# Unit 0 in two halves of heads, an earlier weight piece, unit 5's attention moved with TensorE transposes, and the last tile in halves

## The chip, the core and the metric

The kernel runs on one core of a Trainium2 chip. The metric is the device time of one execution in microseconds; the kernel before took 304.26 us (median of 3 runs, 303.33 to 305.32) when the prediction was made. The "span" of a profile is the time from the first to the last instruction; the device time is about 2 us longer. A profile shows one execution only. In its lines PE is TensorE (PEld its weight loads), DVE VectorE, ACT ScalarE, POOL GpSimd and SP SyncE; L220 is line 220 of that run's kernel. A run is called slow here when it took over 1.5% more than the fastest run of the same kernel.

## The reference, cut to what matters

```python
# q, k, v: (8 batches, 8 heads, 576 positions, 64) fp32; chunks of 64 positions attend to themselves
scores = scale * q_c @ k_c.T                   # 64x64 per chunk and head
attn   = exp(scores - max) / sum
x      = (attn @ v_c) laid out as 4608 tokens x 512
h      = x @ w_in                              # 512 -> 2048
g      = h * sigmoid(beta * h)
out    = g @ w_out                             # 2048 -> 512
```

A *unit* is 256 tokens, a *block* is two units. The names below: `sc` the scores, `et` their exponential, `x` the attention product and its normalised copy, `xt` its transpose, `hps` the first product (16 *groups* m of 128 rows of w_in's output, 4 matmuls each), `gt` the gated result, `ops` the second product. *Scores 5* is the scores of unit 5, h6 the second half of columns of group 6, and a *PSUM tile* is one of the four buffers that groups, transposes and outputs share.

## The kernel before

Attention for the next units is laced between the matmuls of the current block by a list of positions. From block 1's second half on, x is transposed by DMA; the first four units are transposed by TensorE.

```python
    def emit_T(u, which=("kT", "qT")):      # VectorE transposes of k and q, 32x32 blocks
        ...
        loads_to(u + 4)                     # frees buffers: the loads of unit u+4 may go

    def emit_norm(u, s):                    # VectorE: reciprocal, then x * 1/sum -> x16
        ...
    def emit_xt_pe(u, s, on_act=True):      # 4 TensorE transposes, ScalarE copies them to xt
        ...
    def emit_xt_dma(u, s):                  # SyncE: DMA transpose x16 -> xt
        xf = x16_t.pop((u, s)).rearrange("p r h d -> p (r h d)")
        nc.sync.dma_start_transpose(out=xt_at(u, s), in_=xf)

    def emit_m(j, m, c0=0, n=None):         # one group: 4 matmuls, tanh on ScalarE, product on VectorE
        ...                                 # its PSUM tile comes from a pool of 4 (ps_p)

    with tc.manual_schedule():
        # unit 0: two loads by SyncE; the rest by GpSimd, in this order:
        # v of unit 0, q and k of unit 1, v of unit 1, 8 pieces of w_in, w_out, units 2, 3
        ...
        emit_idle(12, 512)                  # warm-up matmuls
        nc.scalar.copy(out=q_t[0], in_=raw0[0])
        nc.vector.tensor_copy(out=k_t[0], in_=raw0[1])
        emit_T(0, ("qT", "kT"))
        emit_sc(0, True)
        ...
        for j in range(1, NB):
            items = []
            if j == 1:
                items += [(0.03 * m, 0, ("h", m)) for m in range(9)]        # second half of columns
                items += [(0.30 + 0.10 * (m - 9), 0, ("m", m)) for m in range(9, KFF)]
                items += [(0.29, 3, ("T", 4))] + att_items(4, 0.45, 0.55)[:-1] + [(0.90, 3, ("T", 5))]
            else:
                m0 = 0.42 if j == 2 else 0.02
                ...
                if j == 2:
                    items += att_items(5, 0.01, 0.40)       # all of unit 5's attention
            ...                                             # emitted in order of position
        for t in range(4):
            emit_t(NB - 1, t)
```

The softmax here doesn't subtract the row's maximum and nothing guards it: scores larger than these inputs give would overflow.

Of the kernel before, what the change touches and what calls it, by code (L numbers as in the profile page):

```python
# [8 lines left out]
FP32 = mybir.dt.float32  # L9
FP16 = mybir.dt.float16  # L10
ACTF = mybir.ActivationFunctionType
ALU = mybir.AluOpType
# [3 lines left out]
def kernel(  # L16
# [14 lines left out]
    CH = 64  # L31
# [22 lines left out]

    ident = const.tile([128, 128], FP16)
    idle = const.tile([128, 512], FP16)
    raw0 = [const.tile([128, H, 2, D], FP32, name=f"raw{i}") for i in range(2)]
    braw = const.tile([128, 32], FP32)
    bt = const.tile([128, 32], FP32)
    beta2 = const.tile([128, KFF], FP32)  # L60
# [46 lines left out]
    def loads_to(u):  # L107
        while nxt[0] <= min(u, NU - 1):
            load_unit(nxt[0])
            nxt[0] += 1  # L110
# [31 lines left out]
    x_t = {}  # L142
    x16_t = {}
    xt_t = {}

    def emit_sc(u, split=False):
        qt, kt = qT.pop(u), kT.pop(u)
# [108 lines left out]
    def emit_idle(n, w):  # L256
        d = ps_p.tile([128, 512], FP32, tag="p", name="warm")
        for _ in range(n):
            nc.tensor.matmul(out=d[:, 0:w], lhsT=idle[:, 0:128], rhs=idle[:, 0:w])  # L259

    with tc.manual_schedule():
        nc.vector.memset(idle, 0.0)
        nc.vector.memset(braw, 0.0)  # L263
        nc.vector.memset(vbig[:, :, :, D:D + 1], 1.0)
        for i, src in enumerate((q, k)):
            nc.sync.dma_start(
                out=raw0[i],
                in_=src[0, :, 0:UNIT, :].rearrange("h (p r) d -> p h r d", r=2),
            )
        bv = moe_beta.rearrange("(m w f) -> w m f", w=4, f=32)  # L270
        for w in range(4):
            nc.sync.dma_start(out=braw[32 * w:32 * w + KFF, :], in_=bv[w])
        for dst, nm in ((q_t, "qu"), (k_t, "ku")):
            dst[0] = qk_p.tile([128, H, 2, D], FP16, tag=nm, name=nm)
        load_v(0)
        load_v(1)
        nxt[0] = 1
        loads_to(1)
        make_identity(nc, ident)
        for g in range(8):  # L280
            load_w_in(g)
        for g in range(3):
            load_w_out(g)
# [1 line left out]
        load_w_out(3)  # L285
        loads_to(3)

        emit_idle(12, 512)
        nc.scalar.copy(out=q_t[0], in_=raw0[0])
        nc.vector.tensor_copy(out=k_t[0], in_=raw0[1])  # L290
        emit_T(0, ("qT", "kT"))
        emit_sc(0, True)
        nc.vector.transpose(out=bt, in_=braw)
        nc.scalar.activation(out=beta2, in_=bt[:, 0:KFF], func=ACTF.Copy, scale=0.5)
        emit_idle(6, 128)
        emit_pv(0)
        emit_norm(0, 0)
        emit_norm(0, 1)
        emit_idle(8, 128)
        emit_xt_pe(0, 0)  # L300
        emit_xt_pe(0, 1)
        emit_T(1)
        emit_sc(1, True)
# [30 lines left out]
        emit_m(1, 0, 0, 256)  # L334
        emit_m(1, 1, 0, 256)
        emit_sc(3, True)
        for m in range(2, 6):
            emit_m(1, m, 0, 256)
        emit_pv(3)
        emit_norm(3, 0)  # L340
        emit_norm(3, 1)
        for m in range(6, 9):
            emit_m(1, m, 0, 256)
        emit_xt_pe(3, 0)
        emit_xt_pe(3, 1)

        def att_items(u, a0, w):
            return [(a0, 2, ("sc", u)), (a0 + 0.40 * w, 3, ("pv", u)),
                    (a0 + 0.41 * w, 3, ("norm", u, 0)), (a0 + 0.55 * w, 3, ("norm", u, 1)),
                    (a0 + 0.70 * w, 3, ("T", u + 1))]  # L350

        for j in range(1, NB):
            items = []
            if j == 1:
                items += [(0.03 * m, 0, ("h", m)) for m in range(9)]
                items += [(0.30 + 0.10 * (m - 9), 0, ("m", m)) for m in range(9, KFF)]
                items += [(0.29, 3, ("T", 4))] + att_items(4, 0.45, 0.55)[:-1] + [(0.90, 3, ("T", 5))]
            else:
                m0 = 0.42 if j == 2 else 0.02
                items += [(m0 + (1 - m0) * m / KFF, 0, ("m", m)) for m in range(KFF)]  # L360
                for t in range(4):
                    for hf in range(2):
                        items.append((0.98 * (t + 0.5 * hf) / 4, 1, ("t", t, hf)))
                if j == 2:
                    items += att_items(5, 0.01, 0.40)
                if j + 1 < NB:
                    if j == 2:
                        items += att_items(6, 0.40, 0.29) + att_items(7, 0.68, 0.26)
                    else:
                        for i in range(2):  # L370
                            items += att_items(2 * j + 2 + i, 0.03 + 0.43 * i, 0.43)
            items.sort(key=lambda it: it[:2])
            for _, _, it in items:
                if it[0] == "m":
                    emit_m(j, it[1])
                elif it[0] == "h":
                    emit_m(j, it[1], 256, 256)
                elif it[0] == "t":
                    emit_t(j - 1, it[1], 8 * it[2], 8 * it[2] + 8)
                elif it[0] == "sc":  # L380
                    emit_sc(it[1])
                elif it[0] == "pv":
                    emit_pv(it[1])
                elif it[0] == "norm":
                    emit_norm(it[1], it[2])
                    emit_xt_dma(it[1], it[2])
                elif it[1] < NU:
                    emit_T(it[1])
        for t in range(4):
            emit_t(NB - 1, t)  # L390


# [28 lines left out]
```

## Time and profile before

| what | value | from |
|---|---|---|
| span of the profiled execution | 303.2 us | head of the page |
| TensorE busy | 285.1 us, 94% | busy table |
| VectorE, ScalarE busy | 151.2, 147.3 us | busy table |
| mean granted clock of TensorE | 0.983 | result of that execution |
| chain that ended last: TensorE's share | 84% | chain of waits |

Two things are to be read from it. TensorE is the bound, and a bound engine can gain only where it stands still or runs slowly. A mean clock of 0.983 means that (1 - 0.983) x 303.2 / 0.5 = 10 us of this execution ran at half clock. Such stretches last 3.4 us or a multiple of it; 3.4 us is called a *window* below. The prediction below shows the lines of the slices, the stretches and the waits that say where.

### The profile page before, as it was taken

The numbers are of one execution on the slowest core, as the hardware profiler recorded it, in microseconds if no ns is written. First come the engines' busy times: TensorE is split into PE (matmuls) and PEld (weight loads), VectorE is DVE, ScalarE is ACT, GpSimd is POOL, SyncE is SP. The second block draws the span as 40 slices with busy tenths as digits, with TensorE's granted clock in tenths as the row PEclk, the third lists the DMA queues.
The fourth block names the chain that finished last, engine by engine and source line by source line (L and its number), as shares of the span: only waits on it lengthen the run. The fifth ranks groups of instructions, "written<-read, shape, count | busy, mean of one in ns | idle before, by whom it ended". The sixth has DMA issues, their size and how long they took to land.

```text
span 303.2 us, 7038 instructions
## 1 busy us (share of the span) xinstructions
PE 285.1 (94%) x2998; PEld 138.7 (46%) x2998; DVE 151.2 (50%) x272; ACT 147.3 (49%) x227; POOL 79.0 (26%) x104
## 2 busy tenths in 40 slices
PE   6789999798399999999999999999999999999995
PEld 2564446644134444444444444444444444444442
DVE  1577424776028755563647364736473635444300
ACT  3387228772227454545454545454545455544411
POOL 8843667644403340504060404000000000000000
PEclk9799999999869999999999999999999999999999
DMA  9999999999963992969196919411120212100011
GB/s 171 182 196 206 178 173 226 185 168 143 186 49 83 111 152 58 132 96 141 52 134 94 140 54 143 85 37 55 51 70 37 67 39 71 66 38 37 35 69 69
DMA packets 102046, 32.44 MB, mean 107 GB/s; under 512 B 89216, under 2 KB 97408, under 8 KB 102016
## 3 DMA queue, kind: packets, MB, share of 16 engines
q0 software_dynamic: 79392, 17.83, 64.2%
q1 hardware_dynamic: 22624, 14.17, 16.4%
q8 instruction: 23, 0.38, 0.5%
q14 instruction: 7, 0.06, 0.1%
HBM read 36.71 MB, written 9.44 MB: 152 GB/s over the span
## 4 chain that ended last, share of the span: by engine, by line
PE 84%; DVE 7%; DMA 4%; ACT 2%; issue 1%; SPq 0%; ACTq 0%; DVEq 0%
PE ops L242 40%; PE hps L220 38%; PE sc L153 4%; DVE gt L229 3%; DMA xt<-x 2%; DMA raw<-in_k_dram 2%; PE x L174 2%; DVE x L186 2%; DVE kT L132 1%; DVE qT L132 1%; ACT sg L228 1%; ACT xt L203 1%; PE xp L201 1%; DVE rd L184 0%; ACT osb L252 0%
## 5 line engine op out<-in xcount | busy, mean ns | idle before, releaser
L229 DVE SCALAR_TENSOR_TENSOR gt<-sg,hps 128x512 f16<-128x512 f32 (+1 forms) x159 | 100.2, 635 | 115.3 <-ACT sg L228 114.4
L220 PE MATMUL hps<-xt,win 128*128 128x512 f16 (+1 forms) x636 | 139.0, 363 | 5.9 <-DMA xt<-x 5.0
L228 ACT ACTIVATE sg<-hps,beta 128x512 f32<-128x512 f32 (+1 forms) x159 | 101.7, 647 | 84.0 <-PE hps L220 84.0
L242 PE MATMUL ops<-wout,gt 128*128 128x512 f16 x576 | 135.5, 382 | 0.0
L220 PEld LDWEIGHTS <-win 128*128 128x128 f16 x636 | 60.3, 98 | 65.3 <-issue 8.0
L242 PEld LDWEIGHTS <-gt 128*128 128x128 f16 x576 | 55.9, 98 | 67.4 <-issue 2.2
L252 ACT ACTIVATE osb<-ops 128x512 f32<-128x512 f32 x36 | 21.5, 597 | 44.8 <-PE ops L242 44.8
L87 POOL DMA_DIRECT2D qu<-in_q_dram x23 | 18.0, 787 | 89.3 <-DVE qT L132 85.4
L95 POOL DMA_DIRECT2D vbig<-in_v_dram x40 | 34.0, 866 | 10.5 <-DMA wout<-in_moe_w_out_dram 3.7
L162 ACT ACTIVATE et<-sc 128x1024 f16<-128x1024 f32 (+1 forms) x21 | 18.6, 901 | 17.6 <-PE sc L153 17.6
L186 DVE TENSOR_TENSOR x<-x,rd 128x512 f16<-128x512 f32 x36 | 24.9, 691 | 1.2
L87 POOL DMA_DIRECT2D ku<-in_k_dram x23 | 18.0, 789 | 2.1 <-DMA win<-in_moe_w_in_dram 1.5
L153 PE MATMUL sc<-qT,kT 32*64 32x64 f16 x1152 | 12.8, 193 | 4.7 <-DVE kT L132 2.7
L153 PEld LDWEIGHTS <-kT 32*64 32x64 f16 x1152 | 10.9, 107 | 12.3 <-DVE qT L132 4.8
L132 DVE STREAM_TRANSPOSE kT<-ku 128x512 f32<-128x512 f32 x18 | 12.7, 703 | 2.3 <-DMA ku<-in_k_dram 2.3
L184 DVE RECIPROCAL rd<-x 128x8 f32<-128x8 f32 x36 | 7.2, 200 | 10.3 <-PE x L174 10.3
L132 DVE STREAM_TRANSPOSE qT<-qu 128x512 f32<-128x512 f32 x18 | 12.1, 672 | 0.0
L174 PEld LDWEIGHTS <-et 64*64 64x64 f16 x576 | 6.5, 110 | 8.2 <-issue 3.7
L174 PE MATMUL x<-vbig,et 64*64 64x65 f16 x576 | 8.8, 198 | 0.8 <-issue 0.6
L259 PE MATMUL warm<-idle 128*128 128x128 f16 (+1 forms) x26 | 7.0, 455 | 1.2 <-DVE braw L263 1.2
L113 POOL DMA_DIRECT2D win<-in_moe_w_in_dram x8 | 6.1, 778 | 0.6 <-DMA ku<-in_k_dram 0.4
L203 ACT COPY xt<-xp 128x512 f16<-128x512 f16 x8 | 4.6, 584 | 2.6 <-PE xp L201 2.5
(18 smaller groups left out, 16.9 us busy)
## 6 DMA issues: line engine op xcount, KB each, us to landing
out_dram<-osb SPq DMA_DIRECT2D x36, 256.0 KB, 2.1
vbig<-in_v_dram POOLq DMA_DIRECT2D x32, 128.0 KB, 6.4
qu<-in_q_dram POOLq DMA_DIRECT2D x11, 256.0 KB, 5.2
ku<-in_k_dram POOLq DMA_DIRECT2D x11, 256.0 KB, 6.2
win<-in_moe_w_in_dram POOLq DMA_DIRECT2D x8, 256.0 KB, 10.1
wout<-in_moe_w_out_dram POOLq DMA_DIRECT2D x4, 512.0 KB, 12.6
qu<-in_q_dram POOLq DMA_DIRECT2D x4, 192.0 KB, 7.0
ku<-in_k_dram POOLq DMA_DIRECT2D x4, 192.0 KB, 7.4
```

The lines of the kernel that those rows point to most:

```text
L87: nc.gpsimd.dma_start(out=t[off // 2:(off + n) // 2], in_=src[b, :, s:s + n, :].rearrange("h (p r) d -> p h r d", r=2),)
L95: nc.gpsimd.dma_start(out=vbig[off:off + n, i, :, 0:D], in_=v[b, :, s:s + n, :].rearrange("h p d -> p h d"),)
L132: nc.vector.transpose(out=t.rearrange("p h s e -> p (h s e)").bitcast(FP32).rearrange("p (h i r) -> p h r i", h=H, r=2), in_=a.rearrange(" ...
L153: nc.tensor.matmul(out=sc[o0:o0 + 64, c // 2, h, :], lhsT=kt[p0:p0 + 32, h, :, e], rhs=qt[p0:p0 + 32, h, :, e], start=(e == 0), stop=(e == 1),
L162: nc.scalar.activation(out=et[:, s], in_=sc[:, s], func=ACTF.Exp, scale=scale)
L174: nc.tensor.matmul(out=x[64 * c:64 * c + 64, r, g, 0:D + 1], lhsT=et[64 * r:64 * r + 64, s, 4 * c + g, :], rhs=vbig[64 * r:64 * r + 64, i, ...
L186: nc.vector.tensor_tensor(out=x16, in0=x[:, :, :, 0:D], in1=rd.to_broadcast([128, 2, 4, D]), op=ALU.mult)
L220: nc.tensor.matmul(out=hps[:, 0:n], lhsT=w_in16[m // 2][:, kk, (m % 2) * 128:(m % 2) * 128 + 128], rhs=xr[:, c0 // CH:(c0 + n) // CH, 2 * ...
L228: nc.scalar.activation(out=sg[:, 0:n], in_=hps[:, 0:n], func=ACTF.Tanh, scale=beta2[:, m:m + 1])
L229: nc.vector.scalar_tensor_tensor(out=gt_t[j][:, m, c0:c0 + n], in0=sg[:, 0:n], scalar=1.0, in1=hps[:, 0:n], op0=ALU.add, op1=ALU.mult,)
L242: nc.tensor.matmul(out=ops, lhsT=gt_t[j][:, kk, t * 128:(t + 1) * 128], rhs=w_out16[kk // 4][:, kk % 4, :], start=(kk == 0), stop=(kk == K ...
L252: nc.scalar.activation(out=osb, in_=ops, func=ACTF.Copy, scale=0.5)
```

## The change

Its intent has four parts: start earlier by loading and transposing unit 0 in two halves of heads; bring the first weight piece ahead of unit 1's v; take unit 5 off the late DMA transpose by moving its attention (scores in block 1, the rest at the head of block 2, transposes on TensorE); end earlier by copying and storing the last tile in two halves.

```diff
+    def emit_T_half(a):       # casts and transposes of 4 heads
+    def emit_sc_half(a):      # scores and exponential of 4 heads
...
-        for i, src in enumerate((q, k)):
-            nc.sync.dma_start(out=raw0[i], in_=src[0, :, 0:UNIT, :]...)
+        for a in range(2):
+            for i, src in enumerate((q, k)):
+                nc.sync.dma_start(out=raw0[a][i], in_=src[0, HH * a:HH * a + HH, 0:UNIT, :]...)
...
-        nxt[0] = 1
-        loads_to(1)
+        load_qk(1)
+        load_w_in(0)
+        load_v(2)
+        load_v(3)
...
-        emit_idle(12, 512)
-        ...
-        emit_sc(0, True)
+        emit_idle(10, 512)
+        emit_T_half(0)
+        emit_sc_half(0)
+        emit_idle(8, 128)
+        emit_T_half(1)
+        emit_sc_half(1)
...
-        for m in range(2, 6):                # block 1, first half of columns: unit 3's product
+        for m in range(2, 5):                # one group earlier,
...
-        for m in range(6, 9):
+        for m in range(5, 10):               # two groups more before the second half
...
-                items += [(0.29, 3, ("T", 4))] + att_items(4, 0.45, 0.55)[:-1] + [(0.90, 3, ("T", 5))]
+                items += [(0.05, 3, ("T", 4)), (0.25, 2, ("sc", 4)), (0.42, 3, ("pv", 4)),
+                          (0.43, 3, ("norm", 4, 0)), (0.50, 3, ("norm", 4, 1)), (0.58, 3, ("T", 5)),
+                          (0.85, 3, ("sc", 5))]
...
-                    items += att_items(5, 0.01, 0.40)
+                    items += [(0.01, 3, ("pv", 5)), (0.02, 3, ("norm", 5, 0)), (0.06, 3, ("norm", 5, 1)),
+                              (0.13, 3, ("xp", 5, 0)), (0.19, 3, ("xp", 5, 1)), (0.20, 3, ("T", 6))]
...
-        for t in range(4):
+        for t in range(3):
             emit_t(NB - 1, t)
+        for hf in range(2):                  # last tile: 2 x 16 matmuls of 256 columns,
+            ...                              # copies on ScalarE and VectorE, stores by SyncE and ScalarE
```

More of the change, by code (lines that the diff above doesn't have):

```diff
@@ L56 @@
     idle = const.tile([128, 512], FP16)
-    raw0 = [const.tile([128, H, 2, D], FP32, name=f"raw{i}") for i in range(2)]
+    HH = H // 2
+    raw0 = [[const.tile([128, HH, 2, D], FP32, name=f"raw{i}{a}") for i in range(2)] for a in range(2)]
+    qk0 = [[const.tile([128, HH, 2, D], FP16, name=f"h0{i}{a}") for i in range(2)] for a in range(2)]
+    qkT0 = [[const.tile([128, HH, CH, 2], FP16, name=f"t0{i}{a}") for i in range(2)] for a in range(2)]
     braw = const.tile([128, 32], FP32)
@@ L144 @@
     xt_t = {}
+    def emit_T_half(a):
+        nc.scalar.copy(out=qk0[a][0], in_=raw0[a][0])
+        nc.vector.tensor_copy(out=qk0[a][1], in_=raw0[a][1])
+        for i in (0, 1):
+            nc.vector.transpose(
+                out=qkT0[a][i].rearrange("p h s e -> p (h s e)").bitcast(FP32).rearrange(
+                    "p (h i r) -> p h r i", h=HH, r=2),
+                in_=qk0[a][i].rearrange("p h r d -> p (h r d)").bitcast(FP32).rearrange(
+                    "p (h r i) -> p h r i", h=HH, r=2),
+            )
+    def emit_sc_half(a):
+        if a == 0:
+            et_t[0] = et_p.tile([128, 2, H, CH], FP16, tag="et", name="et")
+            x_t["s0"] = ps_s.tile([128, 2, H, CH], FP32, tag="s", name="sc")
+        sc = x_t["s0"]
+        qt, kt = qkT0[a]
+        for h in range(HH):
+            for e in range(2):
+                for c in range(4):
+                    p0, o0 = 32 * c, 64 * (c % 2)
+                    nc.tensor.matmul(
+                        out=sc[o0:o0 + 64, c // 2, HH * a + h, :],
+                        lhsT=kt[p0:p0 + 32, h, :, e],
+                        rhs=qt[p0:p0 + 32, h, :, e],
+                        start=(e == 0),
+                        stop=(e == 1),
+                    )
+        hs = slice(HH * a, HH * a + HH)
+        nc.scalar.activation(out=et_t[0][:, :, hs], in_=sc[:, :, hs], func=ACTF.Exp, scale=scale)
     def emit_sc(u, split=False):
@@ L264 @@
         nc.vector.memset(vbig[:, :, :, D:D + 1], 1.0)
-        for i, src in enumerate((q, k)):
-            nc.sync.dma_start(
-                out=raw0[i],
-                in_=src[0, :, 0:UNIT, :].rearrange("h (p r) d -> p h r d", r=2),
-            )
+        for a in range(2):
+            for i, src in enumerate((q, k)):
+                nc.sync.dma_start(
+                    out=raw0[a][i],
+                    in_=src[0, HH * a:HH * a + HH, 0:UNIT, :].rearrange("h (p r) d -> p h r d", r=2),
+                )
         bv = moe_beta.rearrange("(m w f) -> w m f", w=4, f=32)
@@ L272 @@
             nc.sync.dma_start(out=braw[32 * w:32 * w + KFF, :], in_=bv[w])
-        for dst, nm in ((q_t, "qu"), (k_t, "ku")):
-            dst[0] = qk_p.tile([128, H, 2, D], FP16, tag=nm, name=nm)
         load_v(0)
         load_v(1)
-        nxt[0] = 1
-        loads_to(1)
+        load_qk(1)
+        load_w_in(0)
+        load_v(2)
+        load_v(3)
+        nxt[0] = 2
         make_identity(nc, ident)
-        for g in range(8):
+        for g in range(1, 8):
             load_w_in(g)
@@ L286 @@
         loads_to(3)
-        emit_idle(12, 512)
-        nc.scalar.copy(out=q_t[0], in_=raw0[0])
-        nc.vector.tensor_copy(out=k_t[0], in_=raw0[1])
-        emit_T(0, ("qT", "kT"))
-        emit_sc(0, True)
+        emit_idle(10, 512)
[4 more added lines that the diff above has]
+        emit_sc_half(1)
         nc.vector.transpose(out=bt, in_=braw)
         nc.scalar.activation(out=beta2, in_=bt[:, 0:KFF], func=ACTF.Copy, scale=0.5)
-        emit_idle(6, 128)
+        loads_to(4)
+        emit_idle(8, 128)
         emit_pv(0)
@@ L298 @@
         emit_norm(0, 1)
-        emit_idle(8, 128)
+        emit_idle(12, 128)
         emit_xt_pe(0, 0)
+        emit_idle(4, 128)
         emit_xt_pe(0, 1)
@@ L341 @@
         emit_norm(3, 1)
-        for m in range(6, 9):
+        for m in range(5, 10):
             emit_m(1, m, 0, 256)
         emit_xt_pe(3, 0)
+        emit_m(1, 10, 0, 256)
         emit_xt_pe(3, 1)
@@ L354 @@
             if j == 1:
-                items += [(0.03 * m, 0, ("h", m)) for m in range(9)]
-                items += [(0.30 + 0.10 * (m - 9), 0, ("m", m)) for m in range(9, KFF)]
-                items += [(0.29, 3, ("T", 4))] + att_items(4, 0.45, 0.55)[:-1] + [(0.90, 3, ("T", 5))]
+                items += [(0.04 * m, 0, ("h", m)) for m in range(11)]
+                items += [(0.44 + 0.11 * (m - 11), 0, ("m", m)) for m in range(11, KFF)]
+                items += [(0.05, 3, ("T", 4)), (0.25, 2, ("sc", 4)), (0.42, 3, ("pv", 4)),
+                          (0.43, 3, ("norm", 4, 0)), (0.50, 3, ("norm", 4, 1)), (0.58, 3, ("T", 5)),
+                          (0.85, 3, ("sc", 5))]
             else:
-                m0 = 0.42 if j == 2 else 0.02
+                m0 = 0.27 if j == 2 else 0.02
                 items += [(m0 + (1 - m0) * m / KFF, 0, ("m", m)) for m in range(KFF)]
@@ L364 @@
                 if j == 2:
-                    items += att_items(5, 0.01, 0.40)
+                    items += [(0.01, 3, ("pv", 5)), (0.02, 3, ("norm", 5, 0)), (0.06, 3, ("norm", 5, 1)),
+                              (0.13, 3, ("xp", 5, 0)), (0.19, 3, ("xp", 5, 1)), (0.20, 3, ("T", 6))]
                 if j + 1 < NB:
                     if j == 2:
-                        items += att_items(6, 0.40, 0.29) + att_items(7, 0.68, 0.26)
+                        items += att_items(6, 0.32, 0.34) + att_items(7, 0.66, 0.30)
                     else:
@@ L385 @@
                     emit_norm(it[1], it[2])
-                    emit_xt_dma(it[1], it[2])
+                    if it[1] != 5:
+                        emit_xt_dma(it[1], it[2])
+                elif it[0] == "xp":
+                    emit_xt_pe(it[1], it[2])
                 elif it[1] < NU:
                     emit_T(it[1])
-        for t in range(4):
+        for t in range(3):
             emit_t(NB - 1, t)
+        for hf in range(2):
+            ops = ps_p.tile([128, DM], FP32, tag="p", name="ops")
+            for kk in range(KFF):
+                nc.tensor.matmul(
+                    out=ops[:, 0:256],
+                    lhsT=gt_t[NB - 1][:, kk, 384:512],
+                    rhs=w_out16[kk // 4][:, kk % 4, 256 * hf:256 * hf + 256],
+                    start=(kk == 0),
+                    stop=(kk == KFF - 1),
+                )
+            osb = osb_p.tile([128, DM], FP32, tag="osb", name="osb")
+            dst = out[NT - 128:NT, 256 * hf:256 * hf + 256]
+            if hf == 0:
+                nc.scalar.activation(out=osb[:, 0:256], in_=ops[:, 0:256], func=ACTF.Copy, scale=0.5)
+                nc.sync.dma_start(out=dst, in_=osb[:, 0:256])
+            else:
+                nc.vector.tensor_scalar(out=osb[:, 0:256], in0=ops[:, 0:256], scalar1=0.5, scalar2=None, op0=ALU.mult)
+                nc.scalar.dma_start(out=dst, in_=osb[:, 0:256])
 _INS = ['q', 'k', 'v', 'moe_w_in', 'moe_w_out', 'moe_beta']
```

## The prediction

> **What bounds the kernel now.** I read the busy table and the 40 slices first, then the waits, then the timeline around every place where TensorE isn't solid.
>
> ```profile
> PE   6789999798399999999999999999999999999995
> ...
> PEclk9799999999869999999999999999999999999999
> ```
>
> Each digit is a fortieth of 303.2 us, 7.58 us. From slice 13 (about 91 us) TensorE is full at full clock, so nothing can be won there except by removing work. The loss lies in the first slices and in the eleventh (75.8 to 83.4 us), where TensorE is busy 3 tenths; the granted clock is 8 and 6 tenths there and in the next slice. Busy time by stretch makes it exact (columns: length, busy time and count of PE, PEld, DVE, ACT, POOL, then clock, DMA share, GB/s):
>
> ```profile
> 60.00:77.00 17.00, 15.70 (x315) 7.70 (x312) 11.81 (x23) 8.01 (x12) 8.69 (x11) 1.00 1.71 162
> 77.00:82.10 5.10, 0.07 (x9) 0.03 (x1) 0.00 (x0) 1.09 (x2) 2.59 (x3) 0.91 1.79 165
> 82.10:88.50 6.40, 6.40 (x17) 2.25 (x18) 1.37 (x2) 1.37 (x2) 0.00 (x0) 0.54 1.13 102
> 88.50:96.00 7.50, 7.50 (x69) 3.31 (x71) 5.39 (x11) 4.03 (x6) 0.07 (x1) 1.00 0.18 45
> ```
>
> TensorE stands still for 5.0 us, then runs 17 matmuls of 512 columns in 6.40 us at about half clock. At the usual pitch (64 take 13.83 us in the chain: 0.216 us each) they'd take 3.67 us, so the hole costs 5.03 + 2.73 = **7.8 us**. The chain of waits names what ended it:
>
> ```profile
> 75.63 6.33 DMA xt<-x
> 81.97 0.14 issue
> 82.10 3.57 PE hps L220 x8
> ```
>
> That is unit 5's second transpose, by DMA. It needed 6.33 us to land where the median is 2.4 us (table of DMA issues), in a stretch whose DMA share is 1.79, with loads of unit 10 in flight. Block 2's first product needs it and nothing is left to run meanwhile. The waits between 45 and 90 us show the small ones:
>
> ```profile
> PE hps L220 <- DMA xt<-x: 5.0, 1, 5.0
> PE sc L153 <- DVE qT L132: 1.3, 2, 0.8
> PE xp L201 <- ACT xt L203: 0.7, 1, 0.7
> PE hps L220 <- ACT xt L203: 0.7, 1, 0.7
> ```
>
> At the start the chain is latency, not throughput:
>
> ```profile
> 1.26 5.70 DMA raw<-in_k_dram
> 6.98 0.78 DVE ku L290
> 7.76 0.62 DVE qT L132
> 8.38 0.60 DVE kT L132
> 9.03 0.77 PE sc L153 x64
> ```
>
> **What the Trainium skill says.** "TensorE: Matmul & The Clock Gate", Part 1: the clock falls to half after about one idle window of 3.4 us and comes back after a busy one; the windows run freely. The trace agrees: half clock from about 81.2 to 88.05 us, two windows. The same page, Architectural detail, says VectorE and ScalarE run their queues strictly in order, while TensorE only pulls weight loads ahead. The trace fits: the second transpose of unit 3 (54.45 us) started only after the product of group m = 6 (ended 54.42), which stood in VectorE's queue behind unit 3's normalisation. I use this below. "DMA: Bandwidth & Descriptors", Anatomy of one DMA, gives a fixed cost of about 2.0 us; this case's output stores take 2.1 us for 256 KB, so halving the last store saves only tenths.
>
> **The change part by part.**
>
> *First unit in halves.* In the trace q landed at 5.08 and k at 6.98 us. With half the heads each, q and k of the first half are as many bytes as q alone, so they should be there at about 5.1; the first half's scores fit under the second half's landing. After that landing remain half a cast (0.4), two half transposes (0.7), half the scores (0.4) and half an exponential (0.55) in place of 0.78 + 1.33 + 0.77 + 1.09: the attention product starts near 9.7 instead of 10.48 us. But 12 + 4 warm-up matmuls (about 0.1 us each) replace 8 ahead of the two transposes, so half of the 0.8 us goes back. More important, what follows waits for weights. The third group of the first block (m = 2) starts at 17.00, and GpSimd's wait for the second w_in piece ends at 16.98, the third at 18.04. Moving the first piece ahead of two v tiles brings that piece from about 14.5 to about 12 us, but the second piece has the same bytes ahead of it as before. Only the waits after 17.0 can go: 0.28 us before the second transpose of unit 1 and 0.24 us before the next groups, of which I count **0.2 us**.
>
> *End of block 1's first half.* Unit 3's normalisation comes after 5 products on VectorE (6 before), with 5 groups issued after the attention product (3 before). Four PSUM tiles serve groups and transposes, so the fifth group (m = 9) waits for the product of m = 5, which now stands behind both normalisations: 52.05 + 2 x 0.86 = 53.77, + 0.36 = 54.13, while TensorE is through at 52.9 to 53.0: 1.1 us. Then 0.9 us until unit 3's second copy ends and the second half of the columns starts, at about 56.73. Before, 1.65 us of waits and a start at 55.50 with two groups (0.86 us) fewer done: a loss of 1.23 - 0.86 = **0.4 us**.
>
> *Block 1's second half.* I count from H, its start, with the trace's pitches: TensorE 0.43 (256 columns) and 0.86 (512), ScalarE 0.44 and 0.69, exponential 1.02, VectorE 0.36 and 0.63 back to back, 1.33 for a pair of transposes, 0.86 for a normalisation. VectorE does h0 and h1 from H + 1.14 to 1.95, unit 4's transposes to 3.28, h2 at 3.63. Groups h2 to h5 fill the four tiles, so h6 starts at 3.65; scores 4 4.1 to 4.75, exponential to 5.87, then ScalarE's h7 to h10 to 7.6; VectorE follows: h10 8.03, normalisation 8.9, m11 9.5, normalisation 10.3, m12 10.9, unit 5's transposes 12.18. TensorE has done m14 at 10.4 and **waits 1.8 us** for scores 5. Then scores 12.87, m15 13.75, 8 output matmuls 15.48, attention product of unit 5 15.93, 8 more 17.66, eight TensorE transposes 18.45 (both normalisations end at 17.6), 8 output matmuls 20.2, by which time the copies (three ScalarE pieces of 0.6 from 17.75) have ended at 19.5. Block 2 starts at H + 20.2 = 76.93, or 76.73 with the 0.2 us of the start.
>
> *What that is worth.* At 88.47 us the old kernel has done 40 output matmuls of block 1, scores 6 and the first two groups of block 2. The new one at 76.73 lacks two groups (1.73), scores 6 (0.65) and 16 output matmuls (3.45): 82.56. Gain **5.9 us**, start included: the 7.8 us of the hole and the old small waits, less about 5 us of new waits and 0.8 us of transposes on TensorE. From there on the order is the same and TensorE is full in both.
>
> *Last tile in halves.* 32 matmuls of 256 columns: in the run of 64 that took 11.41 us, 40 of 512 leave 0.115 each, so 3.68 against 3.46 us: +0.2. The last copy is half as long (about 0.4 on VectorE against 0.60) and the last store carries 128 KB: -0.3. Net **-0.1 us**.
>
> Sum: 304.26 - 5.9 - 0.1 = **298.2 us**.
>
> **The rivals.**
>
> 1. *VectorE isn't late at scores 5.* Its work from H to the end of unit 5's transposes is 9.9 us without holes, TensorE's 9.3; my 12.2 contains the first latency (1.14) and a hole behind the exponential. If those overlap better than I walked them, the 1.8 us shrinks to about 0.5, and with the 1.1 us at m = 9 also smaller the time is 296. For it: the positions look tuned. Against: VectorE's strict order, as seen at unit 3.
> 2. *The clock drops in the new wait.* 1.8 us of idleness and 64 short matmuls fall near one window. At the start 2.66 us of idleness before such matmuls sufficed to halve the clock from about 9.6 to 12.9 us. If it happens, a window at half speed adds 1.7 us, two add 3.4: 300 to 301.5. The idle share is smaller than there, so I give it one chance in five.
> 3. *The hole moves to unit 4.* Its transposes remain DMAs, issued at about 65.7 and 67.2 us beside the loads of unit 8. At 6.3 us they'd land by 75, and block 2 wants them at 76.7. Slack of 2 us; a landing of 8 us or more would cost 1 or 2.
> 4. *The start gains its whole 0.8 us*, if the second weight piece lands earlier too: 297.6. I see no reason in the bytes.
>
> **The range and the chances.** The walk over some thirty steps may be off by 1 us either way, rival 1 pulls down by 2, rivals 2 and 3 up by 2 to 3. So 8 in 10 for 295.8 to 300.8. Faster by over 2% means below 298.2, which is my middle: 0.52 for faster, as rival 1 is a little likelier than 2 and 3 together, 0.47 within 2%, 0.01 slower.
>
> **What would show it.** The 5.0 us wait for the DMA should be gone and the clock at 1.00 from 60 to 100 us; scores 5 should wait 1 to 2 us for VectorE's transposes; group m = 9 of block 1 about 1 us; block 2 should start near 76.7 us and the solid stretch should end near 293.8 (299.5 - 5.9 + 0.2). Group m = 2 of block 0 should still start near 17 us, with the first scores near 6.5. I am wrong if the third group starts before 16.3, if the wait at scores 5 is under 0.5 us, if the clock falls after 60 us, or if unit 4's DMA appears in TensorE's waits.

## The result and the profile after

The changed kernel took **300.22 us** (median of 4 runs, 299.54 to 300.56), the kernel before 304.31 us (4 runs). A ratio is the mean time of one kernel's fast runs over that of the other's of the same rounds, so it is not quite the ratio of the medians: here 0.9863, 95% interval 0.9826 to 0.9899, within 2%. That lies in the predicted range of 295.8 to 300.8, 2.0 us above its middle.

The profiled execution took 299.54 us, span 297.7, mean clock 0.994. The slices of the page, busy tenths and granted clock:

```profile
PE   6689999787999999999999999999999999999995
...
PEclk9799999999999999999999999999999999999999
```

The slice with 3 tenths is gone, and so are the two with a clock of 8 and 6. What remains is 7, 8, 7 in slices 8 to 10 (52 to 74 us). The same stretches as in the prediction (length, busy time and count of PE, PEld, DVE, ACT, POOL, then clock, DMA share, GB/s), with the one before them:

```profile
60.00:70.00 10.00, 7.64 (x183) 4.63 (x185) 8.49 (x20) 6.47 (x12) 5.17 (x7) 1.00 2.01 167
...
77.00:82.10 5.10, 5.10 (x86) 2.50 (x85) 2.00 (x3) 2.98 (x4) 3.10 (x4) 1.00 1.35 154
82.10:88.50 6.40, 6.40 (x61) 2.95 (x60) 2.75 (x6) 3.02 (x5) 0.00 (x0) 1.00 0.75 98
```

Between 77 and 88.5 us TensorE now does nothing but work at full clock. In exchange it is idle 2.36 us between 60 and 70, where it was idle 1.30 us before (busy for 8.70 of these 10 us). Three of its waits up to 100 us (those of the first scores, 4.2 us in all, are part of the start below; the others are 1.2 us or less):

```profile
...
PE hps L254 <- DVE gt L263: 1.9, 2, 1.1
PE sc L187 <- DVE qT L135: 1.8, 2, 1.6
PE hps L254 <- ACT xt L237: 1.2, 2, 1.0
```

No DMA is in the list of TensorE's waits. VectorE is the new releaser, at m = 9, h6 and scores 5, three places that the prediction had walked. The timeline of TensorE there (start, length, line, operands, count, wait before it and its releaser; only the lines with a wait, and the first group of block 2):

```profile
54.95 0.60 PE L254 MATMUL hps<-xt,win 128*128 128x256 f16 x4 [1.12 <-DVE gt L263]
...
57.43 2.78 PE L254 MATMUL hps<-xt,win 128*128 128x256 f16 x24 [1.01 <-ACT xt L237]
...
61.01 0.60 PE L254 MATMUL hps<-xt,win 128*128 128x256 f16 x4 [0.79 <-DVE gt L263]
...
69.59 0.71 PE L187 MATMUL sc<-qT,kT 32*64 32x64 f16 x64 [1.56 <-DVE qT L135]
...
77.22 1.89 PE L254 MATMUL hps<-xt,win 128*128 128x512 f16 x8
```

From the start of block 1's second half (57.43) to block 2 (77.22) are 19.8 us; the prediction's walk had 20.2.

The start went the other way. The chain of waits of the changed kernel:

```profile
2.34 6.63 DMA raw<-in_k_dram
8.97 0.02 issue
8.99 0.43 DVE h L151
9.42 0.69 DVE t L153 x2
10.11 0.04 issue
10.16 0.45 PE sc L170 x32
```

The second half of k landed at 8.97 us; the whole k had landed at 6.96 before. The second half's scores began at 10.16 us, when all scores had already been begun at 9.03 before. Where block 0 takes up the second half of its columns, the loss can be read: first the kernel before, then the changed one (lines of the timeline up to 24 us).

```profile
20.14 4.08 PE L220 MATMUL hps<-xt,win 128*128 128x256 f16 x30 [0.24 <-ACT xt L203]
```

```profile
20.91 3.43 PE L254 MATMUL hps<-xt,win 128*128 128x256 f16 x27 [0.24 <-ACT xt L237]
```

The start is 0.77 us longer instead of 0.2 us shorter. In both executions the clock was at half for one window of the start (9.5 to 12.95 us before, 11.0 to 14.4 after), so this pair compares like with like.

### The profile page after: what moved, and what is told of

The parts are those of the page before. It is cut to its first block, busy times and chain, and to the rows that moved or that the text cites. A ratio compares the mean times of both kernels' runs of the same rounds, so it can differ in the third digit from the quotient of the medians.

```text
span 297.7 us, 7145 instructions
## 1 busy us (share of the span) xinstructions
PE 282.3 (95%) x3046; PEld 141.8 (48%) x3046; DVE 151.8 (51%) x278; ACT 148.6 (50%) x232; POOL 79.1 (27%) x104
## 4 chain that ended last, share of the span: by engine, by line
PE 88%; DVE 5%; DMA 2%; ACT 2%; issue 1%; SPq 0%; DVEq 0%; ACTq 0%
PE ops L276 41%; PE hps L254 39%; PE sc L187 4%; DMA raw<-in_k_dram 2%; PE x L208 2%; DVE gt L263 2%; DVE x L220 1%; PE ops L440 1%; ACT xt L237 1%; ACT sg L262 1%; DVE kT L135 1%; DVE qT L135 1%; PE xp L235 1%; SPq L301 0%; ACT et L196 0%
## 5 line engine op out<-in xcount | busy, mean ns | idle before, releaser
L276 PE MATMUL ops<-wout,gt 128*128 128x512 f16 x560 | 130.9, 379 | 0.0
L276 PEld LDWEIGHTS <-gt 128*128 128x128 f16 x560 | 54.0, 98 | 63.8
L286 ACT ACTIVATE osb<-ops 128x512 f32<-128x512 f32 x35 | 20.9, 597 | 42.1 <-PE ops L276 42.1
L196 ACT ACTIVATE et<-sc 128x1024 f16<-128x1024 f32 (+1 forms) x19 | 17.5, 933 | 11.9 <-PE sc L187 11.9
L187 PEld LDWEIGHTS <-kT 32*64 32x64 f16 x1088 | 10.2, 106 | 8.5 <-DVE qT L135 5.1
L187 PE MATMUL sc<-qT,kT 32*64 32x64 f16 x1088 | 12.1, 192 | 1.8 <-DVE qT L135 1.8
L135 DVE STREAM_TRANSPOSE kT<-ku 128x512 f32<-128x512 f32 x17 | 12.0, 705 | 2.2 <-DMA ku<-in_k_dram 2.2
L135 DVE STREAM_TRANSPOSE qT<-qu 128x512 f32<-128x512 f32 x17 | 11.4, 670 | 0.0
L237 ACT COPY xt<-xp 128x512 f16<-128x512 f16 x10 | 5.7, 586 | 3.0 <-PE xp L235 2.9
```

Of the source, the lines that this page charges most:

```text
L135: nc.vector.transpose(out=t.rearrange("p h s e -> p (h s e)").bitcast(FP32).rearrange("p (h i r) -> p h r i", h=H, r=2), in_=a.rearrange(" ...
L187: nc.tensor.matmul(out=sc[o0:o0 + 64, c // 2, h, :], lhsT=kt[p0:p0 + 32, h, :, e], rhs=qt[p0:p0 + 32, h, :, e], start=(e == 0), stop=(e == 1),
L196: nc.scalar.activation(out=et[:, s], in_=sc[:, s], func=ACTF.Exp, scale=scale)
L276: nc.tensor.matmul(out=ops, lhsT=gt_t[j][:, kk, t * 128:(t + 1) * 128], rhs=w_out16[kk // 4][:, kk % 4, :], start=(kk == 0), stop=(kk == K ...
L286: nc.scalar.activation(out=osb, in_=ops, func=ACTF.Copy, scale=0.5)
```

## The experiments

All twelve gave correct results, and all but one were timed in 5 rounds. Three sets shared their runs of the kernel before: its medians there were 304.69, 305.29 and 305.04 us (11 runs each), and its single runs spread from 301.22 to 306.78 us. Comparisons below are within a set unless it is said otherwise. Medians take in slow runs, ratios only fast ones.

### First set: which part does what

**a1_old_start**: the changed kernel with the old start.

```diff
-    raw0/qk0/qkT0 in halves, emit_T_half, emit_sc_half; first w_in piece ahead of v
+    raw0 whole, emit_T(0), emit_sc(0, True); loads and warm-ups as in the kernel before
```

> The changed kernel with the old start (unit 0 whole, old order of the weight pieces, old warm-ups); unit 5 and the last tile stay changed. Theory: the second half of k landed at 8.99 us against 6.98 for the whole k, so the halves made the start 0.8 us longer (second half of the columns of block 0 began at 20.91 against 20.14 us); this kernel then begins it near 20.1 us and is 0.8 us faster than the changed kernel, about 299.4 us (ratio to the kernel before 0.984). Rival: the late landing was chance of that execution and the halves are worth 0.2 us as predicted; then this kernel is as fast or 0.2 us slower than the changed one.

Measured: 299.61 us (298.71 to 300.09), ratio 0.9827. Against the 300.22 of the first comparison that would be 0.6 us, but the changed kernel repeated in the second set took 299.61 too. In this run's profile the half clock lasted from about 7.6 to 17.8 us, three windows, and the second half of block 0's columns began at 21.32, not at 20.1. So the expectation failed in that profile, and in the medians the new start shows neither gain nor loss. The clock is not held equal in this comparison; the profiles of all runs, sorted by it, are in the account of the start below.

**a2_start_only**: the kernel before with only the new start.

```diff
-    the old start
+    the new start (halves, first w_in piece ahead of v, new warm-ups); the rest as before
```

> The kernel before with only the new start. Theory: k's second half again lands near 9 us and the second half of the columns of block 0 begins near 20.9 us; 0.5 to 1.0 us slower than before, about 305.0 us. Rival (predicted): begins at 19.9, 0.2 us faster, about 304.1. Second rival: the hole at 77 us absorbs nothing, since it moves with the start, so no difference may hide there.

Measured: median 305.72 us (303.44 to 308.51; the two longest of six, 308.17 and 308.51, are rated slow), ratio of the fast runs 0.9997 (0.9936 to 1.0058). The second k was cast at 9.59 us, again late, and the second half of the columns began at 21.88, with two windows of half clock. The time cannot decide: the hole at 77 us scatters it by more than the effect.

**a3_middle_only**: the kernel before with only unit 5's move and its schedule.

```diff
-    for t in range(3): emit_t(NB - 1, t)   # and the last tile in halves
+    for t in range(4): emit_t(NB - 1, t)   # from a1_old_start
```

> The kernel before with only unit 5's move (with the new schedule around it), old start, old tail. Theory: 5.7 to 6.2 us faster than before, 298.4; and within 0.1 us of the first kernel of this set, since the last tile in halves gives -0.1 by prediction and +0.2 for matmuls, -0.3 for copy and store by its parts. Rival: the tail is worth 0.5 us or more, then this one is that much slower than the first kernel of this set.

Measured: 299.66 us (299.13 to 300.51), ratio 0.9839. It is 0.05 us from a1_old_start: the last tile in halves is worth nothing that can be measured, and unit 5's move alone, with the schedule around it, is the whole gain. The gain is 5.0 us by the set's medians, a little under the 5.7 to 6.2 expected. Its second half of block 0's columns began at 20.17, as in the kernel before, with one window of half clock like there.

**s1_two_queues**: the loads of the second halves by ScalarE's queue.

```diff
-                nc.sync.dma_start(out=raw0[a][i], ...)
+                (nc.sync, nc.scalar)[a].dma_start(out=raw0[a][i], ...)
```

> The changed kernel with the loads of the second halves of q and k issued by ScalarE's queue at the same time as the first halves by SyncE's. Theory A (late issue: the second k was issued at 2.34 us against 1.26 for the whole k, and so stands behind more of the other loads): second k lands near 7 to 7.5 us, scores of the second half start near 8.3 to 8.7, and the kernel gains 0.5 to 1 us over the changed one. Theory B (the 16 engines share out bytes whoever issues first, and GpSimd's loads take their part): it still lands near 9 us and nothing is gained.

Measured: 299.84 us (299.51 to 300.02), ratio 0.9836. The timeline of its casts and second scores:

```profile
6.15 0.63 DVE L151 CAST h<-raw 128x512 f16<-128x512 f32 x1 [3.76 <-DMA raw<-in_k_dram]
7.39 0.52 DVE L151 CAST h<-raw 128x512 f16<-128x512 f32 x1
...
8.51 0.61 ACT L150 CAST h<-raw 128x512 f16<-128x512 f32 x1
...
9.98 0.64 PE L170 MATMUL sc<-t,t 32*64 32x64 f16 x32 [1.47 <-DVE t L153]
```

The second cast of k starts at 7.39 us with no wait for its load, so the load had landed by then: it was issued at 1.26 us and landed at about 6.9, where the whole k had landed before. Theory A holds for the landing. (The edit changes the queue along with the time of issue, so it does not part these two; theory B's landing near 9 us is refuted either way.) But nothing is gained. The first k is now 1.1 us later (6.15 against 5.01), and ScalarE, in order, casts the second q only at 8.51, behind the first half's exponential, so the second scores start at 9.98. Of theory A the landing came true and the profit did not.

### Second set: the hole, the clock and VectorE's order

**after_again**: the changed kernel, unedited.

> The changed kernel once more, as a reference for this set and for the spread of its runs. Theory (the clock's windows run freely, so each execution of the kernel before pays the hole with 1, 2 or more half-speed windows, and its times spread from 302.1 to 306.8 us, while the changed kernel has no hole): 299.5 to 300.6 us again, a spread under 1.5 us, in every run a mean clock of 0.985 or more. Rival (the new wait of 1.6 us at scores 5 drops the clock in some runs): single runs near 302 us with a clock below 0.98.

Measured: 299.61 us (298.94 to 300.80), ratio 0.9829 (0.9791 to 0.9868); clocks 0.987 to 0.994. A spread of 1.9 us, somewhat more than the 1.5 expected, but no run near 302 and no clock under 0.985. In its profile the clock is full from 60 to 96 us, as in the first. In these two executions the new wait at scores 5 does not drop it.

**before_filled**: idle matmuls in the hole of the kernel before.

```diff
                 if it[0] == "m":
+                    if j == 2 and it[1] == 0:
+                        emit_idle(20, 512)
                     emit_m(j, it[1])
```

> The kernel before with 20 idle matmuls of 512 columns (20 x 0.216 = 4.3 us) put ahead of block 2's first group, so TensorE works through the hole but still waits for the DMA. Theory: the clock stays at full, the 2.7 us of half-speed matmuls go, and with them the spread: 301.5 to 302.5 us, that is 2 to 3 us faster than the median of before, and no more than 1.5 us between its runs. The wait itself, 5 us, stays. Rival (the half clock costs little, the wait is all): within 0.7 us of before's median and as wide a spread.

Measured: 302.80 us (302.18 to 306.82), ratio 0.9943 (0.9896 to 0.9991). By medians that is 2.5 us faster than the kernel before, as the theory had it, but by the ratio only 1.7; it still waits for the DMA. Four of six runs lie between 302.2 and 303.1. But two runs took 305.62 and 306.82 (the latter rated slow), so the spread did not go. Its profile is the one of 305.62 and shows why: chain of waits first,

```profile
76.05 7.63 DMA xt<-x
83.67 0.14 issue
83.81 2.64 PE hps L220 x8
```

then TensorE's timeline.

```profile
77.11 4.49 PE L259 MATMUL warm<-idle 128*128 128x512 f16 x20
83.81 2.64 PE L220 MATMUL hps<-xt,win 128*128 128x512 f16 x8 [2.21 <-DMA xt<-x]
```

The DMA transpose took 7.63 us in this execution, outlived the filling by 2.2 us, and the clock still fell for one window (half from 84.8 to 88.2 us). So the cost of the hole is a throw of two dice, the landing and the clock's phase.

**m1_early_T4**: the old start, and unit 4's transposes where VectorE idles.

```diff
-                items += [(0.05, 3, ("T", 4)), ...
+                items += [(-0.01, 3, ("T", 4)), ...
```

> The changed kernel with the old start and with unit 4's two transposes ahead of the second half's first product on VectorE, where VectorE idled 1.2 us, rather than after its second. Theory: the 0.8 us wait of group h6 for VectorE's product goes (61.01 us in the changed kernel's profile), and the wait at scores 5 shrinks from 1.6 to about 1.2, so block 2 starts 1.0 us earlier after the start of the second half; about 298.8 us. Rival: VectorE's queue is full anyway and the order doesn't matter: 299.6 us.

Measured: 298.76 us (297.78 to 299.47), ratio 0.9799. That is 0.85 us under the changed kernel of the same set, as expected. The old start came back with this edit, but the profile separates the two: from the start of block 1's second half to block 2 are 19.8 us in each of the five profiles with the given order and either start (after, after_again, a1_old_start, a3_middle_only, s1_two_queues), and 18.8 here, 1.0 less as expected. In its waits only one entry of 1.1 us is left for VectorE's products: the 0.8 us of group h6 is gone. The wait at scores 5 stayed at 1.6 us; I had expected 1.2.

**m2_early_T4_T5**: unit 5's transposes too.

```diff
-                          ... (0.58, 3, ("T", 5)),
+                          ... (0.26, 3, ("T", 5)),
```

> As the last, and unit 5's transposes right after scores 4, where VectorE waits 1.2 us for ScalarE's exponential, rather than behind both normalisations of unit 4. Theory: scores 5 no longer waits (0.0 to 0.3 us), another 1.2 us: about 297.5 us. Rival: loads of unit 9 are then issued some 4 us earlier and meet unit 4's DMA transposes, which land late, and TensorE waits for them ahead of block 2 instead: 299 us or more.

Measured: **297.89 us** (297.22 to 298.77), ratio 0.9772 (0.9738 to 0.9806), the best of all kernels here and faster than both given ones. TensorE's waits from 40 to 100 us:

```profile
PE hps L220 <- DVE gt L229: 1.1, 1, 1.1
PE hps L220 <- ACT xt L203: 1.0, 1, 1.0
PE hps L220 <- DMA xt<-x: 0.6, 1, 0.6
```

The wait at scores 5 is gone, and from the second half to block 2 are 18.0 us, 0.9 fewer than in m1_early_T4. The medians give 0.87 us against 1.2 expected, since the rival is partly true: unit 4's DMA transposes now take 6.9 and 8.5 us to land and hold block 2 for 0.6 us.

### Third set: the start's clock, the order once more, and what makes the DMA late

**m3_warm_start**: m2_early_T4_T5 with more warm-up matmuls.

```diff
-        emit_idle(12, 512)
+        emit_idle(18, 512)
```

> The last middle version (old start, both transposes early) with 18 in place of 12 warm-up matmuls of 512 columns ahead of the first scores: 18 x 0.427 us at half clock end at 8.9 us, just before the scores can start. Theory: TensorE's 2.6 us of idleness before the first scores is what lets the clock fall, for one to three windows, up to 18 us; without it the clock stays full, mean clock of all runs 0.994 or more, second half of block 0's columns starts at 20.0 to 20.3 us in every run; 0.5 us faster than without, about 297.3 us, with a spread under 0.8 us. Rival: the sparse work from 9 to 14 us drops the clock anyway, later: no gain, or a loss where the drop reaches further into the weight products.

Measured: 298.49 us (298.33 to 299.05), ratio 0.9818; clocks 0.983 to 0.994. The theory fell. The idle time ahead of the first scores shrank to 1.14 us, but the clock dropped later, and in the profiled execution onto the weight products: 8 matmuls that take 1.05 us in the kernel before took

```profile
17.21 1.89 PE L220 MATMUL hps<-xt,win 128*128 128x256 f16 x8
```

and the second half of the columns began at 21.26. The rival holds, somewhat later than it said: in the window before the drop, 12.9 to 16.3 us, TensorE was busy for only 1.50 of 3.4 us. The ratio is worse than m2_early_T4_T5's 0.9772 of the second set; no set holds both, so the size of the loss is not measured. The spread did shrink to 0.7 us.

**m4_T5_before_product**: as m3_warm_start, with unit 5's transposes between unit 4's normalisations.

```diff
-                          ... (0.26, 3, ("T", 5)),
+                          ... (0.435, 3, ("T", 5)),
```

> As the last, but unit 5's transposes between unit 4's two normalisations on VectorE instead of right after scores 4. Theory: no wait at scores 5 either (VectorE done at about 67 us), and loads of unit 9 issued 3 us later than in the last, so the 0.6 us wait for unit 4's DMA transposes ahead of block 2 goes; the same as the last or up to 0.6 us faster. Rival: unit 4's second normalisation is 1.3 us later and its DMA transpose with it: the wait for the DMA grows to 1 or 2 us, 0.5 to 1 us slower than the last.

Measured: 298.93 us (298.43 to 299.06), ratio 0.9825. The wait for the DMA is gone, but scores 5 waits 0.7 us for VectorE, which I had not foreseen; by the medians 0.4 us slower than m3_warm_start. Its profile also had three windows of half clock at the start, to 21 us, so the profile alone doesn't rank the two.

**before_late_loads**: the kernel before, unit 10's loads held back.

```diff
-        loads_to(u + 4)
+        if u != 6:
+            loads_to(u + 4)
...
             t = qk_p.tile([128, H, 2, D], FP16, tag=nm, name=nm)
+            if u == 10:
+                nc.vector.memset(t[:, 0, 0, 0:8], 0.0)   # the load must wait for this write
```

> The kernel before, with only the loads of unit 10's q, k (and so v, in order behind them) held back until after unit 7's transposes, some 18 us later, by a small write of VectorE into their tiles; results unchanged. Theory: those loads, issued at 76 to 80 us, are what makes unit 5's DMA transpose land after 6.3 to 7.6 us instead of 2.4; without them it lands near 79 us, the hole is 1 to 2 us, the clock holds: 299.5 to 301 us. Rival: loads of unit 9, issued at 70 to 74 us and still in flight, or the transposes' own queue make it late: the hole stays at 3 us or more and the time at 303 or above.

Measured: 303.36 us (302.25 to 305.87), ratio 0.9993 (0.9933 to 1.0052). The prediction had named "loads of unit 10 in flight" as the company of the late transpose. Without them its chain of waits reads:

```profile
76.30 5.43 DMA xt<-x
81.87 1.89 PE hps L223 x8
```

5.43 us instead of 6.33, still more than twice the median of 2.4. Even that difference can't be put down to unit 10's loads: a2_start_only, which has them in flight (issued from 77.84 us), shows the same landing.

```profile
76.90 5.49 DMA xt<-x
```

So they are not the cause; the rival stands. Unit 9's loads (issued at 71.3 to 74.9 us here) remain the nearest suspects. The record has something near a test of them for unit 4's transposes, which are issued at 65 to 69 us in all these runs. Where unit 9's loads begin at 69.05 us (m1_early_T4), these transposes land after 4.6 and 5.5 us; at 67.96 (m4_T5_before_product) after 5.0 and 7.0; at 64.54 (m3_warm_start) after 7.5 and 8.8; at 64.14 (m2_early_T4_T5) after 6.9 and 8.5. So loads that begin ahead of a transpose go with a late landing, in one execution each. For unit 5's no run takes them away, nor changes SyncE's queue, on which the transposes stand, so its cause stays open.

**before_again**: the kernel before, unedited, one look.

> The kernel before once more, for a second look at its hole. Theory: the DMA's landing and the number of half-speed windows differ from execution to execution; the hole is 3 to 7 us long, followed by 0 to 3 windows of half clock, and the span follows from the two. Rival: the same 5.0 us and two windows again.

Measured: 305.37 us, span 303.3. The hole was 5.3 us, followed by two windows of half clock (80.7 to 87.5 us). Taken alone this execution sides with the rival; with before_late_loads (3.7 us, and no half clock after it) and a2_start_only (3.6 us, one window), which keep unit 5's transpose as it was, the theory fits better.

## Why the prediction was right, and where it was off

**The mechanism was right.** The hole of 5.0 us and the half clock behind it went, and with them 5.5 us of the span (303.2 to 297.7). a3_middle_only shows that this part alone is the gain. The price of the half clock was read a little low: 16 matmuls, not 17, run between 82.10 and 88.47 us, so they cost 6.37 - 3.46 = 2.9 us over the usual pitch, not 2.73. The forecast itself does not use that figure.

**The walk through block 1 was right to a few tenths.** Predicted and measured in the profile: group m = 9 waits 1.1 and 1.12 us; the second half waits for ScalarE's copy 0.9 and 1.01; h6 starts 3.65 and 3.58 after the second half's start; scores 5 waits 1.8 and 1.56; from the second half to block 2, 20.2 and 19.8 us. Every duration and every pitch in it was taken from this kernel's own trace, and VectorE's queue as strictly in order. The wait that the prediction showed for that order doesn't prove it: the profile puts the second transpose of unit 3 (54.45 us) down to ScalarE's copy, which ended at 54.40, within 0.1 us of VectorE's product. m1_early_T4 and m2_early_T4_T5 are better evidence: with the transposes elsewhere in VectorE's order the waits at h6 and scores 5 went and the kernel gained, so these two were real costs. The waits at m = 9 and ahead of the second half stay in all runs and are not tested.

**The start failed.** The step "the first half's scores fit under the second half's landing", with the rest counted from k's old landing at 6.98 us, took for granted that splitting a load leaves the last byte where it was. (Two of its sums don't close either: 6.98 + 0.4 + 0.7 + 0.4 + 0.55 is 9.0, not 9.7; and 8 more warm-up matmuls at 0.1 us give back all of 0.8 us, not half. Neither enters the 0.2 us.) The second k was issued at 2.34 us instead of 1.26, as the fourth load of its queue, and landed at 8.97. s1_two_queues, which issues it at 1.26 us on a second queue, has it landed by 6.9: the place in SyncE's queue is what made it late. Instead of a gain of 0.2 us the profile has a loss of 0.77. The step behind it, that block 0 waits for the weights anyway, came out nearly right, but is not shown: group m = 2 began at 17.40 us (predicted: near 17), with GpSimd's wait for the second weight piece ending at 17.29, yet right behind unit 1's attention product and with no wait for a weight in TensorE's list. In device times the start's effect stays unresolved: a1_old_start with the old start and after_again with the new one have the same median, 299.61 us, in different sets, and the start's half clock, of one to three windows in the profiles, covers it. Sorted by that, the profiles side with a loss. With one window the second half of the columns began at 20.14, 20.15, 20.17 and 20.41 us with the old start and at 20.91 with the new one; with two at 20.61 (old) and at 21.03 and 21.88 (new). Three windows occurred with the old start only (21.07, 21.28, 21.32), which may be why the medians agree; three of eight profiles against none of four don't show it. (Left out: m3 and m4 with more warm-ups; s1_two_queues began at 21.42, with two windows.)

**The last tile** was predicted at -0.1 us and is worth 0.0: in the old profile 16 x 0.216 us before TensorE's last instruction gives 296.0 us for its start, 7.2 us ahead of the end; in the new one it starts at 290.52, again 7.2 us ahead of the end. Its second store, of 128 KB, landed after 2.0 us against the 2.1 of a whole one; the first, by SyncE, after 1.7.

**The sum took its base from one place and its parts from another.** "304.26 - 5.9 - 0.1" subtracts from a median what was measured in one execution, and that execution took 305.14 us. Pairing the two profiled executions, 305.14 - 299.54 = 5.6 us, against 6.0 predicted: -0.2 for the start became +0.8, the middle gave about 0.5 more than its 5.7 (0.4 of it between the second half and block 2), and the tail 0.1 less. That makes 5.4; 0.2 us stay unaccounted for, and it was partly luck that the total came so close: two errors of opposite sign, 1.0 and 0.5 us, partly cancelled. The medians of the comparison differ by only 4.1. Over all sets the kernel before has a median of 305.03 us (37 runs) and the changed one 299.70 (10 runs): 5.3 us. The runs of one kernel came from several rounds, so I give this difference as an orientation only.

**Why the old kernel scatters and the new one does not.** Of 33 runs of the kernel before that list a clock, the 5 with a clock of 0.986 or more took 302.7 us on average, the 9 from 0.980 to 0.983 took 304.4, the 19 below 0.978 took 305.4. The changed kernel's ten runs lie within 1.9 us. The clock's windows run freely, as the prediction cites, and a hole of about one and a half windows can cost one or two of them; the profiles here show none, one and two after the hole. The average costs follow the clock, which before_filled supports by its median, though the fastest of these runs (301.22 us) had a clock of only 0.981; but the landing of the DMA varies as well (5.4 to 7.6 us), and no run holds one still while it moves the other, so how much of the scatter is whose stays open.

**The rivals.** VectorE was late at scores 5, so rival 1 was wrong. Rival 2 did not show: the lowest mean clock of ten runs was 0.987, and both profiles have full clock after 60 us. The traces say that one chance in five was too much: with 1.56 us of waiting, any window of 3.41 us keeps 1.85 us of work, and no window with that much lost the clock in any trace (last section). The emptier place was at m = 9 and behind it: one window there held 1.48 us of work in a3_middle_only, and kept the clock. Rival 3 did not happen in the changed kernel, but it did, with 0.6 us, as soon as m2_early_T4_T5 took away the slack. Rival 4 went the other way. The mistake in the chances was to put the middle of the forecast on the 2% line without asking how far four runs of the old kernel scatter.

## What to carry to other kernels

If a wait is followed by a slow clock, count both, but subtract them from the time of the same execution and ask how much both vary. When a schedule is packed tighter, walk the in-order queue of the second-busiest engine instruction by instruction: here VectorE's order was worth 1.7 us after the change, and moving its transposes into two holes that the profile shows got it back. Splitting a load so that work can start on its first half can delay the second half: here by 2.0 us when it was issued 1.1 us later on the same queue. Issued at once on a second queue it landed in time, but then the first half came 1.1 us later.

## What the Trainium skill lacked or had wrong

- "TensorE: Matmul & The Clock Gate", Part 1, gives the windows and says that gaps of more than about 3.4 us are to be avoided. It does not say how much work in a window keeps the clock, and shorter gaps sufficed here: 2.66 us of idleness followed by 64 short score matmuls preceded the drop at 9.5 us in the kernel before; with this gap cut to 1.14 us (m3_warm_start) the clock fell at 16.3 us all the same. The 14 traces bracket the answer, if each is cut into windows of 3.41 us that are aligned with its own first drop. (They are counted from 4 us on: before that the warm-up matmuls start 0.43 us apart, twice the usual 0.216, while the record still says full clock.) At full clock, 18 windows were followed by half clock; TensorE was busy in them for 0 to 1.56 us. All 1136 others kept it, and all but three of them (1.40, 1.48, 1.48 us) had more than 1.56. At half clock, 14 windows with up to 2.81 us of busy time stayed at half, and 18 with 3.21 us or more were followed by full clock. In these traces, then, about half a window of work kept the clock, and nearly a full window was needed to get it back.
- "DMA: Bandwidth & Descriptors", DMA Transpose (X-bar), lists constraints but no latency under load. The same transpose of a 128x512 tile took 2.4 us from issue to landing at the median of the kernel before; unit 5's second one took 5.4 to 7.6 us in the runs that kept it, and unit 4's up to 8.8 us (m3_warm_start) where the loads of the next unit began ahead of it.
- "VectorE: DVE Perf Modes", The three transpose paths, gives 390 ns for one 128x128 transpose on TensorE. Back to back eight of them took 0.61 us in block 2 of the changed kernel (under 80 ns each), plus 1.07 us for ScalarE's two copies; no page that I found has a rate for transposes in a row.
- No page that I found says that a load split in two by heads and issued in turn on one queue ends later than the whole: the last bytes of k landed at 8.97 against 6.96 us, with the same bytes of q and k in all.
